# Threshold attention and a bilinear ffn: seven block products for the third column group as well

## The chip, the cores and the metric

The kernel runs on one core of a Trainium2 chip. The core has TensorE for matmuls (PE in the profile, its weight loads PEld), VectorE (DVE), ScalarE (ACT), GpSimd (POOL) and SyncE (SP), whose queue issues nearly all DMAs here; 16 DMA engines move the data. [...] The metric is the time of one execution on the device in microseconds, the median of several runs.

## The reference

```python
batch, n_heads, seq, head_dim = (8, 8, 576, 64)        # q, k, v in fp32; tau = 0.02
scores = scale * q @ k.T
thresh = max(scores) - tau                              # per row
scores = where(scores >= thresh, scores, -1e9)
attn = exp(scores - max(scores)) / (sum(...) + 1e-9)
x = (attn @ v), heads side by side                      # (4608, 512)
a = x @ w_a                                             # w_a, w_b: (512, 1536)
b = x @ w_b
out = (a * b) @ w_out                                   # w_out: (1536, 512)
```

All inputs and the output are fp32.

## The kernel before, in words

**Attention.** The 64 heads are worked on in 32 pairs (`pairs`, four to a batch). A pair's 576 query rows are five *units*: four of 128 rows and a tail of 64 (both heads in one tile). One pass of the main loop over `g` is a *slot* and starts one unit: `scores` (L386, TensorE) into two PSUM tiles, their row maxima on VectorE (L393), then in `weigh` the exponential on ScalarE (L414) and on VectorE the mask with the sum (L417), which is the last reader of the two score tiles. The weights are normalised on ScalarE (L436), transposed in blocks of 32 on VectorE (`turn_blocks`, L480), written to DRAM and read back in another order (`turn_back`; `swap`, `tw` and `wT` in the profile). Three slots behind its unit (`PV_LAG`), the product with v is made (`weighted`, L520) into one PSUM tile, and copied into `x`, transposed (L527, L528).

**The ffn.** A *block* is 256 rows of x (two halves of each batch, and a tail block out of four batches: 18 blocks). `x` and `xs` (the same with the two 64-row halves of the partitions exchanged, by GpSimd, `exchange`) feed matmuls of 64x64 quadrants, four of which make one product. The first layer has the 1536 columns of w_a and w_b in three column groups of 512 (`NG`). For the last two groups (`SEVENS = 2`) the block product of two 2x2 matrices (columns of x's rows, halves of w_a beside w_b) is formed from seven products in place of eight (`sevens_of`, L649 on): sums of weight blocks are made once (`first_sums`, GpSimd, L641), differences of x blocks for each block (`x_sums`, L550, four a tile, on GpSimd). The products accumulate in PSUM: a tile `a` through products 1, 6, 7 and 4 (between them ScalarE copies the running value out, L698, L705, L710), `b` for product 2 (read at L702), then `b` for 5 and 3 (L719, L714); products 4 and 3 end in VectorE's and GpSimd's multiplications (L723, L646). For the first group the four plain steps (column tile 0 or 1, w_a or w_b, `plain`, L753; read out by ScalarE at L759 and VectorE at L761) stand between them: the first three behind products 6, 7 and 5, the last at the end. A block's whole first layer is a generator that yields after every few matmuls. The second layer (L810) uses seven products too.

**PSUM.** `banks()` hands out one of four tiles of two banks each. Scores take two, pv one, an ffn product one; a tile comes free when its last reader is done.

**The order of the work** is written out by hand. The slot's program issues scores, then `advance(...)` for a share of the ffn's columns (`PORTIONS` 0.3, 0.35, 0.15, 0.2 of the slot's `pace`), with the other steps between: behind the first portion `weigh`, behind the second `weighted`, if one is due. `pace` spreads the waiting blocks (`backlog()`, `cost()` columns each) over the slots until the next block arrives. `keep_order` makes every engine follow the program's order. `make_room` runs the ffn on until a product is far enough from its ends before pv takes a PSUM tile, and `make_x` until an x tile is free (`XT_BUFS`, tag `xT`, which also holds the raw weights at the start). `exchange_blocks` turns a complete x into a block when no first layer is running.

**DMAs.** From slot 41 on DMAs are posted to a list (`post`, `bulk`), which `passed` empties by TensorE's progress (`PUMP` columns for each `PART` elements, `pump`); groups with the keys `tw` and `wT` go ahead of others of about the same slot, and `flush` issues what is needed now. v is loaded a slot ahead of a pair's first unit into one of four buffers (`load_v`), q and k a few slots ahead. The weights come at the start, `RAWS` pieces at a time plus as many as there are places in `extra`, and are converted from their 64-bit form in the first 15 slots.

**Weight sums.** From slot 22 on (`g > first[HP] + 1`), one `first_sums` is issued at the end of each slot, six in all; a block gets its x differences if `state["first"]` has reached that count when `exchange_blocks` takes it. The fourth sum of each group is made in place when the first such block starts.

Of the kernel before, what the change touches and what calls it, by code (L numbers as in the profile page):

```python
# [24 lines left out]
XT_BUFS = 7  # L25
# [9 lines left out]
RAWS = 4  # L35
# [19 lines left out]
def kernel(  # L55
# [83 lines left out]
    def post(key, *moves):  # L139

        if not state["paced"]:
            for move in moves:
                nc.sync.dma_start(*move)  # L143
        else:
            at = len(bulk)
            if key[0] in ("tw", "wT"):
                while at and bulk[at - 1][0][0] not in ("tw", "wT") and bulk[at - 1][1] >= state["slot"] - 1:
                    at -= 1
            bulk.insert(at, (key, state["slot"], moves))
# [50 lines left out]
    def load_v(i, again=False):  # L200
        b, hp = pairs[i]
        if not again:
            loaded[i]["v"] = loads.tile([P, NSLOT, D], FP32, tag="vm", bufs=HP, name="vm")
# [47 lines left out]
    more_sb = more_u32.bitcast(FP32)  # L251

# [73 lines left out]
    rooms = [t.rearrange("p (n w) -> p n w", n=NR) for t in rooms]  # L326
    load_rows(0, "q", rooms[0])
# [217 lines left out]
    def x_sums(x):  # L545

        t = x_tile("xU").rearrange("p m (k n) -> p m k n", k=2)
        b11, b12, b21, b22 = (x[:, k * 2:k * 2 + 2, n * P:(n + 1) * P] for k in range(2) for n in range(2))
        for m, a, b in ((0, b12, b11), (1, b22, t[:, 0]), (2, b22, b12), (3, b21, t[:, 1])):
            nc.gpsimd.tensor_tensor(t[:, m], a, b, op=ALU.subtract)  # L550
        return t

    def exchange_blocks():
        while complete and not state["layer"] and not blocks:
# [5 lines left out]
            blocks.append(((x, xs) + ((x_sums(x), x_sums(xs)) if state["first"] >= 3 * SEVENS else ()), what))  # L560
# [70 lines left out]

    def first_sums(n, group):

        quarter = [w[:, NG - 1 - group].rearrange("p (z y e) w -> p z y (e w)", z=2, y=2)[:, :, y]
                   for w in (wa_sb, wb_sb) for y in range(2)]
        s1, s2, s4 = ((first_sb, more_sb)[group][:, m * QUARTER:(m + 1) * QUARTER].rearrange("p (z w) -> p z w", z=2)
                      for m in range(3))
        a11, a12, a21, a22 = quarter
        out, a, b, op = ((s1, a21, a22, ALU.add), (s2, s1, a11, ALU.subtract), (s4, a12, s2, ALU.subtract),
                         (a21, a11, a21, ALU.subtract))[n]  # L640
        nc.gpsimd.tensor_tensor(out, a, b, op=op)  # L641

    def sevens_of(x, hg, plain):
# [5 lines left out]

        def quarter(n, y):  # L650
            return [[(wa_sb, wb_sb)[n][:, NG - SEVENS + g, k] for k in (2 * y, 2 * y + 1, 2 * y + HP, 2 * y + HP + 1)]
                    for g in range(SEVENS)]

        def s(m):
            return [[(more_sb, first_sb)[g][:, m * QUARTER + k * CH:m * QUARTER + (k + 1) * CH] for k in range(HP)]
                    for g in range(SEVENS)]
# [4 lines left out]
        def of_t(m):  # L661
            return [z[:, m, e] for z in (t, ts) for e in range(2)]

        products = {1: (quarter(0, 0), of_x(0, 0)), 6: (s(1), of_t(1)), 7: (quarter(1, 0), of_t(2)),
                    5: (s(0), of_t(0)), 2: (quarter(0, 1), of_x(1, 0)), 4: (quarter(1, 1), of_t(3)),
                    3: (s(2), of_x(1, 1))}
        nf = 2 * SEVENS
        whole = nf * HP * P

        def product(m, out, fresh, last):  # L670
            w, moving = products[m]
            left = whole
            for f in range(nf):
                g, y = f // 2, f % 2
                for k in range(HP):
                    for r in range(2):
                        rows = slice(r * D, (r + 1) * D)
                        for c in range(2):
                            w0 = y * P + c * D
                            nc.tensor.matmul(out[c * D:(c + 1) * D, r, f * P:(f + 1) * P],  # L680
                                             w[g][k][rows, w0:w0 + D], moving[k][rows],
                                             start=(fresh and k == 0 and f == 0),
                                             stop=(k == HP - 1 and f == nf - 1),
                                             skip_group_check=True)
                    left -= P
                    if left:
                        yield P, left, whole
# [4 lines left out]
        h0, h1 = (hg[:, :, :, n * P:(n + 1) * P].rearrange("p f r n -> p r f n") for n in range(2))  # L692
        third = [work.tile([P, nf * P], FP32, tag="osb", bufs=OSB_BUFS, name="u3") for _ in range(2)]
        done = P, 0, 0

        a = banks(nf * P, "pab")
        yield from product(1, a, True, False)
        nc.scalar.copy(h0, split(a))  # L698
        yield done
        b = banks(nf * P, "pab")  # L700
        yield from product(2, b, True, True)
        nc.vector.tensor_tensor(h0, h0, split(b), op=ALU.add)  # L702
        yield done
        yield from product(6, a, False, False)
        nc.scalar.copy(h1, split(a))  # L705
        yield done
        yield from plain(0)
        yield from product(7, a, False, False)
        for r in range(2):
            nc.scalar.copy(third[r], a[:, r])  # L710
        yield done
        yield from plain(1)
        yield from product(4, a, False, True)
# [425 lines left out]
```

## Time and profile before

| | |
|---|---|
| median of 3 runs | 1448.35 us (1442.43 to 1450.38) |
| profiled execution, first to last instruction (span) | 1439.3 us; the page gives no other time of it, so its own time is this span and what lies around it |
| median less span | 9.05 us |
| instructions | 77100 |
| TensorE busy | 1386.8 us, 34208 matmuls |
| VectorE, ScalarE, GpSimd busy | 1015.6, 683.9, 480.4 us |
| chain that ended last, by line | 27% L680 (seven products, first layer), 20% L810 (second layer), 19% L753 (plain products), 10% L386 (scores), 10% L520 (pv) |
| DMA | 223.25 MB, mean 155 GB/s |
| mean granted TensorE clock | 0.992 |

A group line of the profile reads: line, engine, operation, out<-in by the program's names, shapes, count; busy time and mean of one; idle time of the engine before it and what ended that. A timeline line has start, duration, engine, line, operation, tiles, shape and count; what stands in square brackets is idle time before it and who ended it. Matmuls overlap, so that the time of a stretch is taken from starts, not by adding durations.

### The profile page before, as it was taken

The page shows a single profiled execution, that of the slowest core. Times are in us where ns is not written, and L with a number is a line of the kernel's source. Part 1 is how long each engine was busy: PE and PEld are TensorE (multiplying, and loading weights), DVE is VectorE, ACT ScalarE, POOL GpSimd, SP SyncE. Part 2 cuts the span into 40 slices and gives each one's busy share as a digit, 9 for nine tenths or more (in the row PEclk, how much of TensorE's full clock was granted, in tenths as well). Part 3 has the DMA queues.
Part 4 walks back from the last instruction along what each step waited for, and adds up shares of the span by engine and source line. Part 5 has one row for each costly group of instructions (what it writes and reads, how often), then busy time and mean ns, then how long its engine had stood idle before and what let it go on. Part 6 is the DMA issues. An engine that isn't in the chain of part 4 may idle for free.

```text
span 1439.3 us, 77100 instructions
## 1 busy us (share of the span) xinstructions
PE 1386.8 (96%) x34208; PEld 1282.4 (89%) x34208; DVE 1015.6 (71%) x2244; ACT 683.9 (48%) x1244; POOL 480.4 (33%) x668
## 2 busy tenths in 40 slices
PE   6888999999999999999999999999999999999998
PEld 5777798988879889989999999898898989999998
DVE  6997778788767877676757786778867776755223
ACT  5876455545545454544444545344535454430110
POOL 2763713415060605132333333240506060605000
PEclk9899999999999999999999999999999999999999
DMA  9975667667755776567545677466755686450000
GB/s 210 252 227 141 173 173 191 182 171 192 202 137 153 176 201 159 152 160 189 147 125 137 159 186 203 118 171 149 207 135 142 164 217 167 121 160 18 3 18 17
DMA packets 327004, 223.25 MB, mean 155 GB/s; under 512 B 171536, under 2 KB 310800, under 8 KB 326672
## 3 DMA queue, kind: packets, MB, share of 16 engines
q1 hardware_dynamic: 324160, 217.74, 58.5%
q8 instruction: 269, 4.41, 1.3%
q10 hardware_dynamic: 2512, 0.59, 0.2%
q14 instruction: 63, 0.52, 0.1%
HBM read 128.58 MB, written 89.65 MB: 152 GB/s over the span
## 4 chain that ended last, share of the span: by engine, by line
PE 88%; DVE 4%; DMA 4%; issue 2%; SPq 2%; ACT 1%; DVEq 0%; ACTq 0%
PE pab L680 27%; PE po L810 20%; PE pab L753 19%; PE sc L386 10%; PE pv L520 10%; PE po L856 1%; DMA wT<-swap 1%; PE tp L461 1%; DVE mx L393 1%; DVE tw L480 1%; SPq L197 1%; DMA raw<-in_moe_w_a_dram 1%; SPq L143 1%; DMA raw<-in_moe_w_b_dram 0%; DVE tw L417 0%
## 5 line engine op out<-in xcount | busy, mean ns | idle before, releaser
L436 ACT ACTIVATE tw<-tw,rcp 128x576 f32<-128x576 f32 x272 | 197.8, 769 | 228.7 <-DVE rcp L430 228.6
L393 DVE TENSOR_REDUCE mx<-sc 128x1 f32<-128x576 f32 x288 | 206.1, 752 | 140.7 <-PE sc L386 115.6
L414 ACT ACTIVATE tw<-sc,bias,scalars 128x576 f32<-128x576 f32 x288 | 239.4, 831 | 9.8 <-ACT bias L413 0.2
L646 POOL TENSOR_TENSOR h<-h,u 128x512 f32<-128x512 f32 x28 | 35.1, 1276 | 604.2 <-DVE h L723 465.4
L810 PE MATMUL po<-wo_sb,h 64*64 64x256 f32 x3264 | 230.8, 377 | 0.0
L417 DVE SCALAR_TENSOR_TENSOR tw<-sc,thr,tw 128x576 f32<-128x576 f32 x288 | 222.6, 797 | 9.7 <-ACT tw L414 9.1
L386 PE MATMUL sc<-kT,qT 64*64 64x288 f32 x2016 | 198.1, 405 | 7.2 <-issue 2.9
L480 DVE STREAM_TRANSPOSE tw<-tw 128x576 f32<-128x576 f32 x272 | 196.0, 754 | 0.8 <-ACT tw L436 0.8
L810 PEld LDWEIGHTS po<-wo_sb,h 64*64 64x64 f32 x3264 | 178.7, 133 | 15.8 <-DVE h L723 0.3
L520 PE MATMUL pv<-wT,vm 64*64 64x160 f32 (+3 forms) x5184 | 181.7, 273 | 7.1 <-issue 4.3
L520 PEld LDWEIGHTS pv<-wT,vm 64*64 64x64 f32 x5184 | 167.7, 134 | 13.9 <-issue 6.8
L810 PE MATMUL po<-sums_u,h 64*64 64x256 f32 x2448 | 169.6, 377 | 0.3 <-DVE h L761 0.3
L779 POOL TENSOR_TENSOR h<-h 128x256 f32<-128x256 f32 x168 | 117.4, 733 | 119.8 <-PE po L810 116.1
L386 PEld LDWEIGHTS sc<-kT,qT 64*64 64x64 f32 x2016 | 119.5, 133 | 31.9 <-issue 10.6
L810 PEld LDWEIGHTS po<-sums_u,h 64*64 64x64 f32 x2448 | 132.2, 133 | 12.5 <-DVE h L761 1.2
L680 PE MATMUL pab<-xU,wb_sb 64*64 64x128 f32 x4096 | 138.5, 270 | 0.1
L680 PEld LDWEIGHTS pab<-xU,wb_sb 64*64 64x64 f32 x4096 | 131.0, 133 | 2.2 <-issue 0.5
L413 ACT ACTIVATE bias<-mx,scalars 128x1 f32<-128x1 f32 x288 | 83.3, 289 | 92.5 <-DVE mx L393 92.3
L680 PE MATMUL pab<-xS,wa_sb 64*64 64x128 f32 x2048 | 113.1, 270 | 1.2 <-issue 1.2
L753 PE MATMUL pab<-xS,wb_sb 64*64 64x256 f32 (+1 forms) x1536 | 102.9, 359 | 4.1 <-issue 4.1
L527 ACT COPY xT<-pv 128x128 f32<-128x128 f32 (+1 forms) x68 | 17.6, 259 | 187.2 <-PE pv L520 152.6
L753 PE MATMUL pab<-xS,wa_sb 64*64 64x256 f32 (+1 forms) x1536 | 101.4, 361 | 0.0
(138 smaller groups left out, 2427.7 us busy)
## 6 DMA issues: line engine op xcount, KB each, us to landing
wT<-swap SPq DMA_DIRECT2D x244, 288.0 KB, 3.8
swap<-tw SPq DMA_DIRECT2D x480, 144.0 KB, 2.9
vm<-in_v_dram SPq DMA_DIRECT2D x128, 72.0 KB, 2.8
swap<-tw SPq DMA_DIRECT2D x128, 72.0 KB, 3.1
kT<-in_k_dram SPq DMA_DIRECT2D x112, 72.0 KB, 3.1
wT<-swap SPq DMA_DIRECT2D x56, 144.0 KB, 2.6
out_dram<-kept SPq DMA_DIRECT2D x30, 256.0 KB, 3.5
qT<-in_q_dram SPq DMA_DIRECT2D x112, 40.0 KB, 2.6
```

Of the source, the lines that this page charges most:

```text
L386: nc.tensor.matmul(sc[j if u < NT else 0][to, c], qT[r, q0:q0 + D], kT[r, c * SH:(c + 1) * SH], start=True, stop=True)
L393: nc.vector.tensor_reduce(mx[:, c], sc[j], axis=AX.XY, op=ALU.max)
L413: nc.scalar.activation(bias[:, j:j + 1], mx[:, j:j + 1], AF.Copy, scale=e_nscale)
L414: nc.scalar.activation(wb[j], sb[j], AF.Exp, bias=bias[:, j:j + 1], scale=e_scale)
L417: nc.vector.scalar_tensor_tensor(out=wv, in0=sb[j], scalar=thr[:, j:j + 1], in1=wv, op0=ALU.is_ge, op1=ALU.mult, accum_out=sums[:, j:j + 1])
L436: nc.scalar.activation(w, w, AF.Copy, scale=rcp[:, j:j + 1])
L480: nc.vector.transpose(w, w)
L520: nc.tensor.matmul(pv[c * D:(c + 1) * D, y], vm[rows, s], wT[y](rows, s), start=(s == 0), stop=(s == NSLOT - 1))
L680: nc.tensor.matmul(out[c * D:(c + 1) * D, r, f * P:(f + 1) * P], w[g][k][rows, w0:w0 + D], moving[k][rows], start=(fresh and k == 0 and f ...
L753: nc.tensor.matmul(pab[c * D:(c + 1) * D, r], w[rows, f // n, k, fs + c * D:fs + (c + 1) * D], moving, start=(k == 0), stop=(k == H - 1))
L779: (nc.vector if state["over"] else nc.gpsimd).tensor_tensor(*a, **kw)
L810: nc.tensor.matmul(po[c * D:(c + 1) * D, r, y], ht[rows, t0:t0 + D], other[rows, f], start=(f == 0), stop=(f == NF // 2 - 1))
```

## The change

The first column group is now made from seven products as well. `sevens_of` has two streams, `main` (groups 1 and 2, PSUM tiles of 512 columns) and `side` (group 0, 256 columns), each with the seven steps of before and its own `a` and `b`, and they are woven: main 1, main 2, main 6, side 1, main 7, side 6, main 4, side 7, side 2, main 5, side 4, side 5, main 3, side 3. The plain steps in this layer are gone. The side stream's read-outs are one instruction each over 512 elements: three copies on ScalarE (h of 1, h of 6, u of 7) and five operations on VectorE (2, 4, 5, 3, and the multiplication behind 3); before, group 0 took two of each.

The sums of the third group have one buffer, `side_sb`. They are formed at start-up in three more slots (nine in all, `SUMS = 3 * NG`), each is stored to DRAM (`side_store`), and each block loads the three in turn, four DMAs of 128x256 fp32 each (`side_load`): the one for product 6 at the start of the layer, for 5 after side 6, for 3 after side 5. The key `s` is put ahead in the list like `tw` and `wT`, and a side product that needs a load flushes it.

To make room, `x_sums` writes one of its four differences into x itself and keeps three in a smaller tile of its own (tag `xU`, two buffers); `XT_BUFS` goes from 7 to 5, and a waiting block counts as two x tiles; `RAWS` goes from 4 to 3, while the new buffer is one more place for raw weights at the start. v has two buffers in place of four: it is loaded one slot behind a pair's first unit, and again two slots behind its third (`second`); for pairs 2 and 3 the first load goes into the `xU` tiles.

```diff
-XT_BUFS = 7
+XT_BUFS = 5
-RAWS = 4
+RAWS = 3
...
-            if key[0] in ("tw", "wT"):
-                while at and bulk[at - 1][0][0] not in ("tw", "wT") and bulk[at - 1][1] >= state["slot"] - 1:
+            if key[0] in ("tw", "wT", "s"):
+                while at and bulk[at - 1][0][0] not in ("tw", "wT", "s") and bulk[at - 1][1] >= state["slot"] - 1:
...
+        if 2 <= i < HP and not again:
+            spare = work.tile([P, 3, 2, P], FP32, tag="xU", bufs=2, name="vm")
...
+        elif i >= HP or not again:
+            loaded[i]["v"] = loads.tile([P, NSLOT, D], FP32, tag="vm", bufs=2, name="vm")
...
-        t = x_tile("xU").rearrange("p m (k n) -> p m k n", k=2)
+        t = work.tile([P, 3, 2, P], FP32, tag="xU", bufs=2, name="xU")
...
+    def side_load(m):
+
+        for k in range(HP):
+            part = slice(k * CH, (k + 1) * CH)
+            post(("s", m), (side_sb[:, part], side_store[m][:, part]))
...
+            if groups == (0,) and m in sums:
+                flush(("s", 3), ("s", sums[m]))
...
+            for f, k in ([(f, k) for f in range(nf) for k in range(HP)] if groups != (0,) else
+                         [(f, k) for k in range(HP) for f in range(nf)]):
...
+                elif m == 2:
+                    b = banks(size, "pab")
+                    yield from product(2, groups, b, True, True)
+                    nc.vector.tensor_tensor(h0, h0, split(b), op=ALU.add)
+                elif m == 6:
+                    a = held["a"]
+                    yield from product(6, groups, a, False, False)
+                    nc.scalar.copy(h1, split(a))
...
+                elif m == 4:
+                    a = held.pop("a")
+                    yield from product(4, groups, a, False, True)
+                    nc.vector.tensor_tensor(h0, h0, split(a), op=ALU.mult)
+                elif m == 5:
+                    b = held["b"] = banks(size, "pab")
+                    yield from product(5, groups, b, True, False)
...
+                if groups == (0,) and m in (6, 5):
+                    side_load({6: 0, 5: 2}[m])
...
+        main, side = stream((1, 2), h_main), stream((0,), h_side)
+        for of, m in ((main, 1), (main, 2), (main, 6), (side, 1), (main, 7), (side, 6), (main, 4), (side, 7), (side, 2),
+                      (main, 5), (side, 4), (side, 5), (main, 3), (side, 3)):
+            yield from of(m)
...
-            if g == first[p] - 1:
+            if g == (first[p] - 1 if p < HP else first[p] + 1) or p >= HP and g == second[p] + 2:
                 load_v(p)
...
-        if g > first[HP] + 1 and not converting and state["first"] < 3 * SEVENS:
+        if g > first[HP] + 1 and not converting and state["first"] < SUMS:
```

## The prediction

> **What bounds the kernel now.** I read the page first, then the waits of TensorE, then timelines of single stretches.
>
> ```profile
> span 1439.3 us, 77100 instructions
> ...
> PE 1386.8 (96%) x34208; PEld 1282.4 (89%) x34208; DVE 1015.6 (71%) x2244; ACT 683.9 (48%) x1244; POOL 480.4 (33%) x668
> ...
> PE 88%; DVE 4%; DMA 4%; issue 2%; SPq 2%; ACT 1%; DVEq 0%; ACTq 0%
> ```
>
> TensorE is busy for 96% of the span and makes up 88% of the chain that ended last. In windows of 72 us its busy time from 216 to 1368 us adds up to 1137 of 1152 us: only 15 us are idle there, at a granted clock of 1.00. So every matmul saved is worth its full time, and every new wait of TensorE costs its full time. The waits of TensorE between 200 and 1300 us say what such a wait would be:
>
> ```profile
> PE sc L386 <- DVE tw L417: 2.5, 3, 2.1
> PE pv L520 <- DVE kept L510: 1.5, 1, 1.5
> ```
>
> Columns: who waited for whom, us in total, times, longest. Both are waits for a PSUM tile that VectorE had not yet read out; there are hardly any, because a fourth tile was nearly always free.
>
> **The products themselves.** The timeline of TensorE around 740 us has both kinds of work back to back: one column group's part of one of the seven products (L680, 64 matmuls of 128 columns), and one plain step (L753, 64 matmuls of 256 columns):
>
> ```profile
> 737.71 0.27 PE L680 MATMUL pab<-xU,first_u 64*64 64x128 f32 x1
> ...
> 737.82 1.85 PE L680 MATMUL pab<-xU,first_u 64*64 64x128 f32 x60
> 739.46 0.38 PE L753 MATMUL pab<-xt,wa_sb 64*64 64x256 f32 x1
> ...
> 741.18 2.05 PE L753 MATMUL pab<-xS,wa_sb 64*64 64x256 f32 x32
> 742.91 0.54 PE L680 MATMUL pab<-xU,wb_sb 64*64 64x128 f32 x10
> ```
>
> 64 matmuls of 128 columns take 739.46 - 737.71 = 1.75 us (27.3 ns each); one plain step, 64 matmuls of 256 columns, takes 742.91 - 739.46 = 3.45 us. Removed per block: four plain steps (two column tiles, two weight matrices), 4 x 3.45 = 13.8 us. Added: seven products of 64, 7 x 1.75 = 12.25 us. Gain 1.55 us a block.
>
> [...]
>
> How many blocks? 16 of 18 use seven products now (16 multiplications at L723). The planner forms the x differences of a block only when all weight sums are issued. The six sums are issued one a slot from slot 22 (`g > first[HP] + 1`, with first[HP] = 20); the third block's x is complete in slot 30 (unit 27 plus PV_LAG), where no block is running, so it starts at once. With nine sums the ninth is issued at the end of slot 30, after that. So the third block falls back to plain products for all groups and loses the 2 x 1.55 = 3.1 us it has now. Sum on TensorE: 15 x 1.55 - 3.1 = **-20.2 us**. (If the block kept its sums it would be -24.8.)
>
> **PSUM.** There are four tiles. Scores take two, from the first score to the second masked multiplication (L417), 6.5 us in the median of a slot of some 8.4 us. Before, one accumulator is held (`a` through products 1, 6, 7, 4; then `b` through 5, 3), so one tile is spare. In the change the main and the side stream each hold one for most of the layer: `a` of main and `a` of side together from side 1 to main 4, `a` of side with main's `b`, then both `b`. Main 5 takes a new tile directly behind side 2, and side 5 directly behind side 4. With the scores holding two, the only candidate is the tile that VectorE must still read out. Behind it TensorE's whole queue waits: the products, the next scores and pv. What VectorE's latency is, the timeline of VectorE shows; the fifth product ends here at 614.8 us, just behind a unit's scores:
>
> ```profile
> 614.17 1.42 DVE L393 TENSOR_REDUCE mx<-sc 128x1 f32<-128x576 f32 x2 [1.38 <-PE pab L680]
> 615.63 0.23 DVE L394 TENSOR_SCALAR thr<-mx,scalars 128x2 f32<-128x2 f32 x1
> 615.76 1.43 DVE L480 STREAM_TRANSPOSE tw<-tw 128x576 f32<-128x576 f32 x2
> 617.12 1.25 DVE L719 TENSOR_TENSOR u<-u,pab 128x512 f32<-128x512 f32 x2
> 618.29 0.80 DVE L417 SCALAR_TENSOR_TENSOR tw<-sc,thr,tw 128x576 f32<-128x576 f32 x1
> ```
>
> The read-out stands behind two reductions and two transposes and ends 3.6 us after the product (617.12 + 1.25). Today nobody waits for it. I went through 37 such read-outs (L719, L761) between 300 and 1250 us, and took for each the time from the product's end to its read-out or to the first score tile's release, whichever is earlier, and zero if the scores were gone. Within 3 us of the scores' start: 2.8 us in the mean (12 rows); 3 to 6 us: 0.8 (16 rows); later: 0.1. The slot gives 30, 35 and 35% of its ffn columns to these stretches (PORTIONS), so 0.3 x 2.8 + 0.35 x 0.8 + 0.35 x 0.1 = 1.16 us for each of the two allocations. 13 of the 15 blocks run beside attention (the last two don't). Ends: 0, if a tile is always found, and 13 x (2 x 1.28 + 2 x 0.39) = 43 us: 1.28 is the plain mean of the 37, 0.39 their mean excess over 1.75 us, for the two allocations with one side product as cover (side 2 behind main 4, the second layer behind side 3). I take 0.85 for each of the 26, **+22 us**: a quarter below 1.16, because while TensorE waits VectorE runs ahead and the next read-out comes sooner (estimate).
>
> [...]
>
> **ScalarE's read-outs.** Product 7 adds into the tile that ScalarE still copies out after product 6 (L705), and 4 after 7 (L710). Now a plain step of 3.45 us covers each; then one side product of 1.75 us. The copies of L705 end 1.1 us after the product in 12 or so of 16 blocks, and 4.3, 2.8 and 3.1 us in three; L710's 1.2 us, and twice 3.1. Excess over 1.75: (4.95 + 2.7)/16 = 0.48 us a block, 6 us in 13. Bounds 0 (scores or pv fall between) and 6; I take **+4**.
>
> **Side loads.** Three times a block, four DMAs of 128 KB on SP's queue. The load for side 6 is posted at the block's start and that for side 5 five products ahead: both hidden. That for side 3 is posted when side 5 ends, with only main 3 (3.5 us) between. SP issues four DMAs in 1.75 us:
>
> ```profile
> 704.34 1.75 SPq L156 DMA_DIRECT2D swap<-tw  x4
> 708.41 3.49 SPq L156 DMA_DIRECT2D wT<-swap  x4
> ```
>
> and swap<-tw, 144 KB, the nearest size, lands 2.9 us after its issue. The quarters land 3.3, 3.8, 4.2 and 4.7 us after side 5; side 3 (k outermost) wants them at 3.5, 3.9, 4.4 and 4.8. That is in time by 0.1 to 0.2 us, and late by 1.75 or 3.5 us if a group of tw or wT issues stands ahead, unless scores or pv (1.4 to 2.4 us) fall between. Bounds 0 and 13 x 3.5 = 45; nearest to the plain case, 0.45 us a block: **+6**.
>
> **Together, with small answers.** VectorE gets five read-outs of some 0.67 us for two, +2 us a block, and ScalarE one of 0.58: 30 and 9 us beside 29% and 52% idle; their latency is in the terms above. The multiplication behind side 3 is hidden by the second layer's first product (48 matmuls of 53.9 ns, 2.6 us) against 1.4 us of VectorE; uncovered it would cost 1.4 us a block. v is loaded again for 28 pairs (112 more DMAs on SP), and 180 side loads come in: with 1152 packets a pair and 512 a load some 55,000 packets on 327,004, 17% more; the DMA share of some 0.65 in the windows from 216 us on becomes about 0.76. TensorE waits 0.4 us for a wT now; the loads stand three slots ahead of their use: 0, and 5 us at worst. The three stores of sums hold SP's queue behind GpSimd's sums of 2.4 us in slots 28 to 30, with kT, qT, tw and wT behind them: 0 to 7, I take **+1**. x_sums and the h product stay. XT_BUFS 7 to 5 leaves the same room beside a block (7 - 4 = 5 - 2 = 3); RAWS 3 and one more place in `extra` keep four pieces in flight: 0, at worst 3 us in the first 144 us, where TensorE is idle for 32.
>
> Sum: -20.2 + 22 + 4 + 6 + 1 = **+12.8 us** on a span of 1439.3, 1452.1. The median of the runs is 9.05 us above this span, and what lies around it doesn't change: 1448.35 + 12.8 = 1461.
>
> **The rivals.** *The spare tile isn't missed* (ends faster): the two allocations fall behind the scores' release, which 35% of the columns already do at 0.1 us. Then -20.2 + 4 + 2 remain, 1434; it decides when waits of all kinds stay below 13 us (20.2 less the 7.2 us that can be told). For it speaks that the planner shapes the phases; against it that the fifth product ended within 3 us of the scores in 7 of 12 blocks of that stretch. *The waits just pay for the gain*: 1441 to 1455. *The last side load is late as well*: banks at 1.28 us for each of the 26 (33) and 1.5 us a block for the load (20): -20 + 33 + 6 + 20, 1487; for it speaks the margin of 0.1 us, against it attention's work between. *Fewer blocks than 15*: each costs 4.7 us more; nothing after slot 31 speaks for it.
>
> **How the numbers follow.** Half a per cent, 7.2 us, is about what can be told from no change. Forecast 0.47, late loads 0.08: slower 0.55. Even 0.15. Spare tile 0.30: faster. The range goes from 1429 (the spare-tile case with the ScalarE copies hidden too) to 1483; about one in ten lies outside on each side. The forecast's own range is 1456 to 1475.
>
> **What the profile after would show.** 34208 + 15 x 192 - 384 = 36704 matmuls; 15 blocks with seven products, the third plain; TensorE's busy time down by some 20 us. New waits PE pab <- DVE at the starts of main 5 and side 5, some 20 us in total; PE pab <- ACT of a few us; PE pab <- DMA side_u before side 3. If the idle time from 216 us on stays near 15 us, the bank term was wrong and the time is near 1434. If idle is up by over 50 us, it is the loads.

## The result, and the profile after

The changed kernel takes 1549.55 us (median of four runs, 1540.53 to 1552.42) against 1448.13 us before: 1.0707 times the time before, 95% interval 1.0661 to 1.0754. It is 101 us slower. The forecast was 13 us slower, with a range that ended at 1483: the sign was right, the size wrong by a factor of eight. The two executions that were profiled, and that all step times below come from, differ by a little more: spans of 1439.3 and 1547.2 us, 107.9 us apart.

The page of the changed kernel has these lines for those shown of before:

```profile
span 1547.2 us, 82699 instructions
...
PE 1409.6 (91%) x36704; PEld 1258.8 (81%) x36704; DVE 1038.4 (67%) x2276; ACT 691.4 (45%) x1259; POOL 490.6 (32%) x674
...
PE 75%; DVE 8%; DMA 6%; issue 5%; ACT 2%; SPq 2%; POOL 0%; DVEq 0%; ACTq 0%
```

The count of matmuls is the forecast 36704: 15 blocks have seven products in all groups, and the third block is plain. In columns streamed from 216 us on, TensorE's work fell from 1167.1 to 1146.9 us at full speed, by the forecast 20.2 us. But its share of the chain fell from 88 to 75%, and idle time from 216 us on rose from 15.0 to 97.6 us. The waits of TensorE between 200 and 1400 us (who for whom, us in total, times, longest):

```profile
PE pab L701 <- issue: 25.5, 27, 2.7
PE pab L701 <- DVE h L752: 15.7, 7, 2.9
PE pab L701 <- DMA side_u<-side_store: 14.7, 8, 6.2
PE pab L701 <- DVE tw L424: 9.7, 8, 3.4
...
PE pab L701 <- ACT h L740: 1.5, 1, 1.5
```

L701 is the seven products, L752 the multiplication that reads the side stream's (or the main stream's) `a` behind product 4, L424 the mask that frees the scores, L740 a copy by ScalarE. All three forecast waits are there, and one that has no name: "issue". Two stretches of the timeline:

```profile
895.89 0.75 DVE L400 TENSOR_REDUCE mx<-sc 128x1 f32<-128x576 f32 x1
...
896.27 0.86 PE L701 MATMUL pab<-xU,wb_sb 64*64 64x128 f32 x24
...
896.81 1.43 DVE L487 STREAM_TRANSPOSE tw<-tw 128x576 f32<-128x576 f32 x2
...
898.16 1.25 DVE L758 TENSOR_TENSOR u<-u,pab 128x512 f32<-128x512 f32 x2
899.33 0.68 DVE L752 TENSOR_TENSOR h<-h,pab 128x512 f32<-128x512 f32 x1
...
900.06 1.69 PE L701 MATMUL pab<-xU,side_u 64*64 64x128 f32 x40 [2.93 <-DVE h L752]
...
1235.73 0.62 PE L701 MATMUL pab<-xS,first_u 64*64 64x128 f32 x16
1235.81 1.05 SPq L156 DMA_DIRECT2D wT<-swap  x2
1236.96 1.97 SPq L156 DMA_DIRECT2D swap<-tw  x4
1239.02 1.98 SPq L156 DMA_DIRECT2D side_u<-side_store  x4
...
1242.52 0.87 PE L701 MATMUL pab<-xT,side_u 64*64 64x128 f32 x9 [6.17 <-DMA side_u<-side_store]
```

In the first, side 4 has ended at 897.1 and side 5 wants a PSUM tile. The scores hold two, the main stream's `b` one, and the fourth is the one that side 4 has just filled. VectorE reads it only behind a reduction, two transposes and the read-out of main 5. In the second, main 3 ends at 1236.3 and side 3 wants its sums. Their four DMAs stand behind six others on SP's queue, are issued from 1239.02 on, and TensorE idles 6.17 us.

What follows such an idle time is seen in windows around the first stretch (window, length, busy time of PE with its matmuls, PEld, DVE, ACT, POOL; then the granted clock, the DMA share, GB/s):

```profile
892.00:897.00 5.00, 5.00 (x170) 4.64 (x160) 1.91 (x5) 2.40 (x4) 0.00 (x0) 1.00 0.97 265
897.00:900.00 3.00, 0.13 (x7) 0.00 (x0) 3.00 (x6) 1.18 (x3) 0.00 (x0) 1.00 0.94 271
900.90:904.20 3.30, 3.30 (x72) 3.30 (x68) 1.93 (x4) 0.00 (x0) 0.00 (x0) 0.50 0.49 82
904.30:908.00 3.70, 3.70 (x123) 3.29 (x117) 0.50 (x2) 0.27 (x1) 0.00 (x0) 1.00 0.56 134
```

After the idle 2.93 us the clock is granted at 0.50 for 3.4 us. The engine counts as busy there, with 72 matmuls in 3.30 us, where 123 are made in 3.70 us later. From 216 us to the end of the last products this happens ten times, for 37.5 us in all, so 18.8 us of work are lost; before it never happened in that stretch.

To see where the time went, I summed for each step the time from one matmul's start to the next one's, less 0.2117 ns a column (27.1 ns for 128 columns, the spacing in undisturbed stretches), with the scores and pv that fall into the step. Mean of the first 13 seven-product blocks, us of delay a block, worked out from the two traces:

| step | before | after |
|---|---|---|
| main 5, side 5 (each takes a tile) | 0.21 | 1.44, 2.55 |
| side 3 (late load) | none | 1.82 |
| main 7, main 4, side 7 | 0.26, 0.06, none | 0.75, 1.03, 0.60 |
| main 1, 2, 6, 3 | 1.49 | 2.03 |
| side 1, 6, 2, 4 | none | 1.47 |
| plain steps | 0.76 | none |
| second layer | 0.61 | 0.82 |
| sum | 3.39 | 12.50 |

13 x (12.50 - 3.39) = 118 us; less 20 us of work it leaves 98 of the 107.9 us between the two traces. The rest lies outside these blocks. Of the 118, the two tiles have 49, side 3 has 24, and all else together 46. The delay of a step includes the half clock that falls into it.

### The profile page after: what moved, and what is told of

Its sections match the earlier page's. It is cut to its first block, busy times and chain, and to the rows that moved or that the text cites. A ratio compares the mean times of both kernels' runs of the same rounds, so it can differ in the third digit from the quotient of the medians.

```text
span 1547.2 us, 82699 instructions
## 1 busy us (share of the span) xinstructions
PE 1409.6 (91%) x36704; PEld 1258.8 (81%) x36704; DVE 1038.4 (67%) x2276; ACT 691.4 (45%) x1259; POOL 490.6 (32%) x674
## 4 chain that ended last, share of the span: by engine, by line
PE 75%; DVE 8%; DMA 6%; issue 5%; ACT 2%; SPq 2%; POOL 0%; DVEq 0%; ACTq 0%
PE pab L701 31%; PE po L862 17%; PE sc L393 9%; PE pv L527 9%; PE pab L807 7%; DVE mx L400 2%; DVE tw L487 2%; DMA side_u<-side_store 1%; PE po L908 1%; DVE tw L424 1%; DMA kT<-in_k_dram 1%; DMA vm<-in_v_dram 1%; SPq L156 1%; DMA wT<-swap 1%; ACT tw L421 1%
## 5 line engine op out<-in xcount | busy, mean ns | idle before, releaser
L424 DVE SCALAR_TENSOR_TENSOR tw<-sc,thr,tw 128x576 f32<-128x576 f32 x288 | 223.7, 799 | 13.2 <-ACT tw L421 13.1
L862 PE MATMUL po<-wo_sb,h 64*64 64x256 f32 x3264 | 221.3, 379 | 0.7 <-DVE h L765 0.7
L862 PEld LDWEIGHTS po<-wo_sb,h 64*64 64x64 f32 x3264 | 159.8, 134 | 28.1 <-DVE h L765 1.0
L862 PE MATMUL po<-sums_u,h 64*64 64x256 f32 x2448 | 158.2, 377 | 2.4 <-DVE h L770 2.3
L393 PEld LDWEIGHTS sc<-kT,qT 64*64 64x64 f32 x2016 | 109.8, 133 | 47.5 <-issue 12.6
L701 PE MATMUL pab<-xS,wa_sb 64*64 64x128 f32 x2880 | 139.7, 270 | 0.3 <-issue 0.3
L862 PEld LDWEIGHTS po<-sums_u,h 64*64 64x64 f32 x2448 | 115.3, 133 | 26.5 <-DVE h L770 4.9
L701 PE MATMUL pab<-xT,wa_sb 64*64 64x128 f32 x2496 | 124.1, 270 | 3.4 <-DVE h L752 1.8
L701 PEld LDWEIGHTS pab<-xS,wa_sb 64*64 64x64 f32 x2880 | 114.3, 133 | 2.5 <-issue 1.4
L701 PEld LDWEIGHTS pab<-xT,wa_sb 64*64 64x64 f32 x2496 | 101.5, 133 | 6.3 <-DVE h L752 2.1
L701 PE MATMUL pab<-xU,wb_sb 64*64 64x128 f32 x2880 | 94.9, 270 | 6.6 <-issue 5.7
```

What stands on the lines that cost most here:

```text
L393: nc.tensor.matmul(sc[j if u < NT else 0][to, c], qT[r, q0:q0 + D], kT[r, c * SH:(c + 1) * SH], start=True, stop=True)
L424: nc.vector.scalar_tensor_tensor(out=wv, in0=sb[j], scalar=thr[:, j:j + 1], in1=wv, op0=ALU.is_ge, op1=ALU.mult, accum_out=sums[:, j:j + 1])
L862: nc.tensor.matmul(po[c * D:(c + 1) * D, r, y], ht[rows, t0:t0 + D], other[rows, f], start=(f == 0), stop=(f == NF // 2 - 1))
```

## The experiments

Three theories at the start: **B**, a PSUM tile is missing where main 5 and side 5 take one; **L**, the loads of side 3 are late; **M**, the edits for memory (v loaded twice, fewer x tiles) and the traffic of the loads slow down everything else.

Each interval compares a run with the kernel before as it ran beside it, at 1442.4 to 1443.9 us; beside the changed kernel it had 1448.1. A difference between a run and the changed kernel therefore carries some 6 us of doubt, and the step times of the traces say more. What is given per block is the mean of 13 blocks, as in the table.

**Order of side 4 and main 5.** The multiplication behind side 4 gets main 5 as cover before side 5 takes its tile.

```diff
-                      (main, 5), (side, 4), (side, 5), (main, 3), (side, 3)):
+                      (side, 4), (main, 5), (side, 5), (main, 3), (side, 3)):
```

> The changed kernel (1549.6 us) with one thing altered: side 4 stands ahead of main 5, so the woven order ends main 4, side 7, side 2, side 4, main 5, side 5, main 3, side 3. Side 5 then no longer takes a PSUM tile directly behind side 4, and main 5 has one side product between it and side 2. Theory B (a product that takes a PSUM tile finds none free, because main and side hold one each and the scores two): TensorE's loss at side 5, 2.5 us a block now, falls below 0.5 us, that at main 5 (1.4) to about 1; main 3 may lose 0.5 to 1 us more since its adds have less cover; 1515 to 1530 us in all. Theory L (late side loads, more DMA traffic) and theory M (fewer x tiles, v loaded twice, three raw tiles): no change beyond 5 us, 1545 to 1555.

1529.09 us, 1.0588 (1.0467 to 1.0708) of before, 20 us less than the change and inside B's forecast. The intervals of the two overlap, so that the size of the gain is not settled by this run; the steps are clearer. The delay at side 5 fell from 2.55 to 0.21 and at main 5 from 1.44 to 0.78 us a block. But main 3 rose from 0.60 to 1.60 (it now finds product 5 not yet read out), and side 3 from 1.82 to 2.94 us. Waits of TensorE in this kernel:

```profile
PE pab L701 <- DMA side_u<-side_store: 25.0, 9, 6.6
PE pab L701 <- issue: 20.0, 29, 3.0
PE pab L701 <- DVE u L758: 7.2, 9, 1.5
```

So B is right in kind: main 5 and side 5 lose 3.0 us a block less, 39 us in 13 blocks, and about half of that comes back as other waits.

**Without the side loads.** The sums of side 6, 5 and 3 are whatever was left in the buffer.

```diff
-            post(("s", m), (side_sb[:, part], side_store[m][:, part]))
+            pass
```

> The changed kernel without the 180 side loads: the side products read whatever lies in the one buffer, so products 6, 5 and 3 of the first column group are made from the wrong sums. Everything else stays. Theory L: side 3's loss (1.8 us a block, 23 us in 13 blocks) goes, and with the DMA traffic also the waits spread over the other products (about 40 us): 1485 to 1525. Theory B: only side 3's own loss goes, 1525 to 1535, and side 5 keeps its 2.5 us and main 5 its 1.4 us a block. Theory M: no change, 1545 to 1555.

1510.47 us, 1.0459 (1.0394 to 1.0524): 39 us less, inside L's forecast. Side 3's delay is gone (0.05 us a block), which is 23 of the 39; the rest came from the other steps, which the loads had also disturbed. The waits for tiles stayed:

```profile
PE pab L701 <- DVE tw L424: 17.3, 11, 2.7
PE pab L701 <- DVE h L752: 16.3, 7, 2.9
```

**Both.**

> The changed kernel with side 4 ahead of main 5 (as in the run with the altered order, 1529) and without the side loads (as in the run without them, 1510; products 6, 5 and 3 of the first column group are made from the wrong sums). If the two causes add up, side 3's loss of 2.9 us a block in the altered order goes as well: 1549.6 - 20.5 - 39 - 13 x 1.1 = 1476, so 1470 to 1492. If the missing tiles are all of it and the loads only fill up what the tiles cost, it stays at 1500 to 1512. What is left above 1448 then belongs to the other joins (main 7 and 4 behind side products, main 3 behind side 5, the second layer's start) and to the plain third block (3 us).

1483.75 us, 1.0292 (1.0241 to 1.0343): 66 us below the change, a little more than 20 + 39. Both causes are there side by side: against the run without loads (1510.47) the order alone now gives 27 us, well outside the spread of either. But 41 us above before remain, although 20 us of work are saved: 60 us of delay that neither B nor L explains. The waits of TensorE that are left:

```profile
PE pab L701 <- issue: 14.5, 23, 1.8
PE pab L701 <- DVE u L758: 8.1, 8, 2.0
```

By steps, main 3 has 15 of the 60 us: in this order it adds onto the tile of product 5 with side 5 alone between. The second layer, which waits for VectorE's last operations on h, has 8. What "issue" is comes below.

**Memory edits alone.** The first group is made by plain steps as before, without the third group's sums and loads; v twice, the smaller x tiles and the other edits stay.

```diff
-        main, side = stream((1, 2), h_main), stream((0,), h_side)
-        for of, m in ((main, 1), (main, 2), (main, 6), (side, 1), (main, 7), (side, 6), (main, 4), (side, 7), (side, 2),
-                      (main, 5), (side, 4), (side, 5), (main, 3), (side, 3)):
-            yield from of(m)
+        main = stream((1, 2), h_main)
+        for m in (1, 2, 6, 0, 7, 0, 4, 5, 0, 3):
+            yield from (main(m) if m else plain())
...
```

> The changed kernel without its side stream: group 0 is made by four plain steps again, in their old places between the main products (six sums, 16 blocks with seven products, no side loads). What stays of the change: 5 x tiles, the differences in a tile of their own with one of them written into x, 3 raw tiles, v with two buffers and loaded twice. The plain steps read the altered x, so group 0's values are not the reference's. Theory M: a good part of the 101 us stays, at least 30: above 1478. Theories B and L: 1446 to 1456, within 8 us of the kernel before, and its waits of TensorE near the 15 us of before.

1447.8 us, 1.0041 (1.0009 to 1.0073), some 6 us. M is out as a main cause. VectorE waits 26 us for q and k loads there and 14.5 us before, and TensorE idles during 1.5 of the 26.

**A tile held in the kernel before.** One more tile is taken ahead of product 4 and read by VectorE behind product 5. No work, load or order of the change is in it.

```diff
+        hold = banks(P, "hold")
+        for c in range(2):
+            nc.tensor.matmul(hold[c * D:(c + 1) * D, 0], wa_sb[0:D, 0, 0, 0:D], x[0:D, 0, 0:P], start=True, stop=True)
...
+        nc.vector.tensor_copy(scalars[:, 6:8], hold[:, 0, 0:2])
```

> The kernel before (1448.1 us) with one PSUM tile taken out of use for two products of each of its 16 blocks: a fifth user takes a tile ahead of product 4, two small matmuls write it, and VectorE reads two columns of it behind product 5. No other part of the change is in it. Two tiles are taken without a spare per block: the held one itself behind plain step 1, and that of product 5 directly behind product 4. Theory B: 2 x 1.0 to 2.0 us in 13 to 14 blocks beside attention, 1475 to 1505 us, with waits of TensorE at the start of product 5. Theories L and M: within 4 us of 1448.

1513.93 us, 1.0483 (1.0417 to 1.0549), 71 us slower and above B's forecast. The waits:

```profile
PE pab L757 <- DVE scalars L723: 21.4, 6, 3.7
PE hold L715 <- DVE h L765: 9.8, 4, 2.8
```

So a missing spare tile costs far more than its place in the sum suggested, in the kernel before as well. The place was not the forecast one: TensorE idles 7 us at the start of product 5, 13 us where the held tile is taken, and 24 us at the plain step behind product 5. While the scores hold two tiles, that step (L757) finds none until VectorE has read the held one, behind both read-outs of product 5. So three tiles in a block lack a spare here, not two, and the 71 us are no direct price for the forecast's term of 22. The half clock comes ten times here too, and takes 22 of the 71 us.

**The side stream in one tile.** Two halves of one tile serve as the side stream's `a` and `b`, so that main and side together hold no more than the four tiles allow; the order is made new so that a side step stands behind each main step.

```diff
-                    a = held["a"] = banks(size, "pab")
+                    if len(groups) > 1:
+                        a = held["a"] = banks(size, "pab")
+                    else:
+                        pair = banks(2 * size, "pab")
+                        a = held["a"] = pair[:, :, 0:size]
+                        held["b"] = pair[:, :, size:2 * size]
...
+        for of, m in ((main, 2), (side, 2), (main, 1), (side, 1), (main, 6), (side, 6), (main, 7), (side, 7), (main, 4),
+                      (side, 5), (main, 5), (side, 4), (main, 3), (side, 3)):
```

> The changed kernel with the side stream in one PSUM tile, products 1, 6, 7, 4 in one half of each bank and 5, 3 in the other, and a new weave: main 2, side 2, main 1, side 1, main 6, side 6, main 7, side 7, main 4, side 5, main 5, side 4, main 3, side 3 (ScalarE copies product 2 first, VectorE adds product 1). Nothing is left out. The side stream then takes one long-lived tile in place of two, every side product has a main product as cover, and the side loads for 5 and 3 have 8.7 us each. Theory B (tiles) with the loads: the loss of 12.5 us a block falls to 4 to 7, the kernel before has 3.4: 1450 to 1480. If the loads or the memory edits were the cause apart from side 3's wait, above 1510.

1532.32 us, 1.0629 (1.0558 to 1.07): a miss, and by the forecast's own words above 1510 speaks for the loads or the memory edits. The delays of the three steps went (main 5 0.61, side 5 0.06, side 3 0.15 us a block), and other waits took their place: main 3 now loses 3.05 us a block to a read-out, and the scores wait for a tile that VectorE has yet to copy into x:

```profile
PE pab L701 <- DVE u L765: 15.6, 9, 5.2
PE sc L393 <- DVE xT L535: 15.1, 5, 6.0
```

The longest of the first kind in the timeline:

```profile
649.74 1.36 PE L701 MATMUL pab<-xU,wb_sb 64*64 64x128 f32 x38
...
654.30 0.78 DVE L361 STREAM_TRANSPOSE kT<-kT 128x576 f32<-128x576 f32 x1 [2.41 <-DMA vm<-in_v_dram]
655.01 1.25 DVE L765 TENSOR_TENSOR u<-u,pab 128x512 f32<-128x512 f32 x2
...
656.31 0.92 PE L701 MATMUL pab<-xT,more_u 64*64 64x128 f32 x12 [5.21 <-DVE u L765]
```

Product 3 adds onto the tile that L765 still has to read behind product 5, with only side 4 (1.75 us) between. And VectorE itself stood for 2.41 us at a transpose whose data was late. From 216 to 1300 us it waits 48 us for loads in this kernel (35 in the changed kernel, 14 before), and TensorE idles during 12 of them. So the late loads have a part in this miss; how large it is was not tested.

**Two weight sums a slot** in that kernel, so that the third block has seven products as well.

```diff
-            first_sums(state["first"] % 3, state["first"] // 3)
-            state["first"] += 1
+            for _ in range(2 if state["first"] < SUMS - 1 else 1):
+                first_sums(state["first"] % 3, state["first"] // 3)
+                state["first"] += 1
```

> As the run with the halved side tile, and two weight sums a slot, so that all nine are issued by slot 26 and the third block, which starts in slot 30, gets its seven products: 16 blocks in place of 15. 3.1 + 1.55 us less on TensorE than with the halved side tile alone, so 2 to 7 us below it; at least 36704 + 384 + 192 = 37280 matmuls.

1523.84 us, 1.057 (1.0504 to 1.0637), 8.5 us below the kernel with the halved tile, somewhat more than the forecast 2 to 7, with two runs each that spread over 6 to 7 us, and 37280 matmuls. The planner's reading of the third block was right; its price is small against the rest.

**A read-out without cover**, in the kernel before: the plain step between products 5 and 3 comes behind product 3. No more tiles are held.

```diff
-        yield from plain(2)
         yield from product(3, b, False, True)
...
-            yield from plain(rest[3:])
+            yield from plain(rest[2:])
```

> The kernel before, with one plain step moved: the one that stood between product 5 and product 3 comes behind product 3. No work, tile, load or buffer is changed, and no more tiles are held than before; product 3 now adds into its tile with nothing between it and VectorE's read-out of product 5. In the trace of before this read-out ends 3.0 us after the product in the mean of the 13 blocks beside attention (39.5 us together) and 1.4 us in each of the last three, 43.7 us in all; the plain step (3.45 us) hides nearly all of it there. Theory C (a read-out without cover costs TensorE its whole latency, whatever the tiles do): less what the scores and pv cover now and then and what VectorE gains by running ahead, 25 to 45 us, and some more where the wait is over 2 us and the clock falls to half: 1470 to 1500 us, waits of PE for DVE at product 3 of 25 to 45 us, around 3 us each. Theory T (only a missing tile costs much; read-outs are taken up by other work in the queue): within 8 us of 1448.

1497.97 us, 1.0374 (1.0343 to 1.0404), 54 us slower. Theory C holds, near the top of its range. Waits of TensorE, and one of them in the timeline:

```profile
PE pab L680 <- DVE u L719: 39.5, 13, 4.6
```

```profile
631.24 1.42 DVE L393 TENSOR_REDUCE mx<-sc 128x1 f32<-128x576 f32 x2 [1.38 <-PE pab L680]
632.70 0.23 DVE L394 TENSOR_SCALAR thr<-mx,scalars 128x2 f32<-128x2 f32 x1
632.83 1.43 DVE L480 STREAM_TRANSPOSE tw<-tw 128x576 f32<-128x576 f32 x2
634.19 1.25 DVE L719 TENSOR_TENSOR u<-u,pab 128x512 f32<-128x512 f32 x2
...
635.49 1.13 PE L680 MATMUL pab<-xT,more_u 64*64 64x128 f32 x16 [3.65 <-DVE u L719]
```

The wait is the whole latency: the read-out ended 39.5 us behind the product in the 13 blocks of the trace of before, and 38 us of idle time stand at product 3 of these blocks now. No gain from "VectorE runs ahead" is seen. The half clock overlaps with 20 us of delay there: each us waited cost half a us more.

**The clock by itself.** TensorE makes equal streams of matmuls and waits between them for a chain of VectorE operations.

```diff
+            for m in range(BUSY):
+                r, c = m // 2 % 2, m % 2
+                nc.tensor.matmul(t[c * D:(c + 1) * D, r, 0:N], w[r * D:(r + 1) * D, c * D:(c + 1) * D],
+                                 u[r * D:(r + 1) * D, :], start=(m < 4), stop=(m >= BUSY - 4))
+            nc.vector.tensor_scalar(u, t[:, 0, 0:N], 1 / (BUSY // 4), None, op0=ALU.mult)
+            for _ in range(chain - 1):
+                nc.vector.tensor_tensor(u, u, u, op=ALU.mult)
```

> None of the reference's work: TensorE alone makes 300 matmuls of the plain step's form (64x64 weights, 256 columns, some 16 us), VectorE reads the sum and makes a chain of 1 to 14 small operations, and the next 300 matmuls wait for the chain's end; each length five times, so 70 idle gaps of TensorE from some 0.4 to 5 us, the output is filled with ones. Theory G (TensorE's clock is halved by the gap itself): as in the traces so far, gaps below 1.5 us are followed by a half clock in at most one of twenty, gaps of 2 to 2.5 us in about half, gaps over 3.5 us always; each time for 3.4 us or twice that. Theory N (the halved clock comes from something else in the kernel, such as the load on the other engines at that moment): no half clock, or one that doesn't go by the gap's length.

(The trace has two records for each matmul of the program, so a stream is 600 records and 32.6 us.) Five streams of one row, each with the idle time ahead of it:

```profile
635.16 32.61 PE L59 MATMUL sums<-u,w 64*64 64x256 f32 x600 [1.54 <-DVE u L64]
669.77 32.61 PE L59 MATMUL sums<-u,w 64*64 64x256 f32 x600 [2.01 <-DVE u L64]
704.85 32.61 PE L59 MATMUL sums<-u,w 64*64 64x256 f32 x600 [2.47 <-DVE u L64]
740.38 34.29 PE L59 MATMUL sums<-u,w 64*64 64x256 f32 x600 [2.93 <-DVE u L64]
778.06 34.29 PE L59 MATMUL sums<-u,w 64*64 64x256 f32 x600 [3.39 <-DVE u L64]
```

After 2.93 us of idle time the same stream takes 1.68 us more. Of all 70 gaps (one execution), none of the 16 below 2.0 us was followed by the half clock, 2 of 10 between 2.0 and 2.5 us, 4 of 5 between 2.8 and 3.0, and all 39 above 3.2; from 5 us on it always lasted 6.8 us in place of 3.4. Theory G holds.

**The waits without a name.** "issue" at L701 is 25.5 us in the changed kernel, some of it in the middle of a product (2.67 us at 380.53, 2.50 us at 722.34), where no tile and no operand is new. For each idle time over 0.3 us with no named releaser (216 to 1300 us) I looked at the packets of the instruction queue that feeds TensorE (206 packets of 16 KB in this stretch). In the changed kernel 17 of 28 end 1.2 to 1.7 us behind the end of such a packet, 16.6 us together; of the 37 idle times with a named releaser 3 do. Before it is 2.5 us, with the memory edits alone 3.0, and without the side loads still 10.2. (Four of the 28, 10.0 us, stand at side 5's first matmul and look like waits for its tile; one of them is among the 17.) A kernel with long streams of matmuls, with and without DMAs beside them, tells whether that is cause or chance:

```diff
+PHASES = tuple((load, cols, again) for again in range(2) for load in (None, "large", "small") for cols in (256, 128))
...
+        for m in range(COUNT[cols]):
+            r, c = m // 2 % 2, m % 2
+            nc.tensor.matmul(t[c * D:(c + 1) * D, r, 0:cols], w[r * D:(r + 1) * D, c * D:(c + 1) * D],
+                             u[r * D:(r + 1) * D, 0:cols], start=(m < 4), stop=(m >= COUNT[cols] - 4))
```

> None of the reference's work: TensorE alone makes long streams of matmuls with nothing to wait for, 100 us each, by turns of 256 columns (the plain step's form, 54 ns a record) and of 128 columns (the side products' form, 27 ns), each once without DMAs, once beside 200 loads of 128 KB in pieces of 1 KB, and once beside 50 loads of 128 KB in pieces of 128 bytes, all twice; the output is filled with ones. In the changed kernel 17 of 28 idle times of TensorE in the middle of its work that no engine explains (16.6 us of 29.7) end 1.2 to 1.7 us after the end of an instruction packet on the queue that feeds TensorE; in the kernel before it is 2.5 us. Theory F (TensorE runs out of instructions, which small matmuls use up twice as fast, when their fetch is held up by DMAs): idle times of 0.4 us and more within the streams of 128 columns beside DMAs, ending 1.2 to 1.7 us after such a packet; at most a few in the streams of 256 columns, and hardly any without DMAs. Theory N (the neighbourhood is chance, and something else of the kernel makes these waits): no idle time over 0.3 us within any stream.

Windows inside the first phases with loads (large pieces with 256 and 128 columns, small pieces with 256 and 128), and the second round's 128 columns without loads; columns as above without ScalarE's:

```profile
215.00:316.00 101.00, 101.00 (x1876) 71.60 (x1872) 0.30 (x4) 0.00 (x0) 1.00 0.80 239
342.00:447.00 105.00, 95.97 (x3309) 90.56 (x3305) 0.00 (x0) 0.00 (x0) 1.00 0.69 204
460.00:563.00 103.00, 103.00 (x1876) 67.81 (x1872) 1.22 (x9) 0.00 (x0) 0.98 0.45 66
570.00:680.00 110.00, 101.27 (x3559) 97.34 (x3555) 1.22 (x9) 0.00 (x0) 1.00 0.37 59
...
787.00:892.00 105.00, 103.85 (x3732) 101.81 (x3728) 0.00 (x0) 0.00 (x0) 1.00 0.02 5
```

The timeline of TensorE in the small-piece phase:

```profile
580.98 3.72 PE L73 MATMUL sums<-u,w 64*64 64x128 f32 x128 [0.85 <-issue]
585.28 3.72 PE L73 MATMUL sums<-u,w 64*64 64x128 f32 x128 [0.57 <-issue]
```

Theory F holds. With 256 columns TensorE is never idle. With 128 columns and no DMAs it loses 1 us in 105, and beside DMAs 9 in 105 or 110; in the second round of phases it is 4.8 and 6.2 us. The idle times stand between runs of 128 matmuls, which with their weight loads are 256 instructions, one 16 KB packet for them (the run with equal streams has 328 such packets for 84,000 matmuls and weight loads, 256 for each). In the four phases beside DMAs 32 of them are over 0.3 us, at 116 packets, and each of these ends 1.2 to 1.65 us behind a packet's end. By that, TensorE has run out of instructions there. The longest is 1.1 us: waits as long as the 2.67 and 2.50 us in the changed kernel were not made here, and no run takes the fetch out of the whole kernel, so that its share there rests on where the idle times stand. (The row of 101.00 us shows that a DMA share of 0.80 does nothing to the large matmuls.)

## Why the prediction was wrong, step by step

Against 33 us of waits in the forecast's sum (22 + 4 + 6 + 1) stand 118 us in 13 blocks. The step that failed is the price of the waits: the terms for PSUM and for the side loads were too small, ScalarE's stood for the wrong cause, and the half clock behind a wait and the instruction fetch were in none.

- **Work, -20.2 us: right**, in columns, matmuls and blocks. But the sign "TensorE's busy time down by some 20 us" failed: it rose by 22.8 us. An engine at half clock counts as busy, which is 18.8 us of this. The other some 24 us (22.8 + 20.2 - 18.8) are, by estimate, waits that the records hide: a matmul's record lasts 0.27 us, while the next one starts 0.027 us later.
- **PSUM, +22 us (bounds 0 to 43): mis-sized, 49.** The places and the mechanism were right. Main 5 cost 1.23 us a block more, near the 1.16 of the prediction's own rows; taking 0.85, "because while TensorE waits VectorE runs ahead", was the first error (the run with product 3 uncovered shows the whole latency paid). Side 5 cost 2.55 us: both allocations were priced alike, by read-outs of the kernel before, but VectorE's queue is fuller behind side 4. In 6 of the 13 blocks main 5's two read-outs (1.25 us) still stand ahead of side 4's, and in the mean side 5 starts 1.8 us behind side 4, while main 5 starts 0.9 us behind side 2. The upper bound of 43 held only idle time. The idle time right before the two products is 40 us; the half clock inside side 5, 7 us, was in no term.
- **Side loads, +6 us (bounds 0 to 45): mis-sized.** Side 3 cost 24 us, and taking all loads away gave 39. The margin of 0.1 to 0.2 us counted a free queue; the stretch at 1235.81 shows six other DMAs ahead. The prediction had named that case, and then took a sum near the plain one. With such a margin the plain case was not the likeliest, and the prediction's rival of late loads (1487) had the better price.
- **ScalarE's read-outs, +4 us (bounds 0 to 6): the wrong cause.** TensorE waits only 2.2 us for the copies at L740 and L746. Yet the steps besides main 5, side 5 and side 3 lost 46 us in sum. Of this, some 10 us (12.1 in these steps, less 2.5 before) are idle times over 0.3 us at the ends of instruction packets; the half clock and late read-outs at other places have shares that were not told apart. No step of the prediction had the instruction fetch.
- **Small matmuls in place of large ones**: in the rows at 740 us two matmuls of 128 columns take 2 x 27.3 ns against 53.9 ns for one of 256, 1.3% more, but a plain step stands beside the small product there. Streams of small matmuls beside DMAs idled for 4 to 9% of the time in the last experiment. The price has to come from a stream, not from one product.
- **Small answers.** Memory edits were costed at 0 to 3 and 0 to 5 us, and measured at some 6: near enough. What they do to VectorE was not looked at: its waits for q and k rose from 14.5 to 35.1 us (216 to 1300 us). Only 3.3 us of that lie under an idle time of TensorE; what a late VectorE costs afterwards was not separated. The DMA share, forecast to go from 0.65 to 0.76, hardly moved: 0.63 before and 0.66 after in the mean from 216 to 1296 us, with 31,752 more packets in place of 55,000.
- **The signs**: "if idle is up by over 50 us, it is the loads" was too narrow. Idle time rose by 82.6 us, and loads were about a third of it (without them it is 25.5 us less).
- **The 9.05 us** between the median and the span were taken as what lies around the span. In every run on record an execution takes only 1.7 to 2.8 us more than its own span, so some 7 us of it are the difference between one execution and the median. The forecast's change of 12.8 us does not depend on it.

What stays open is how the 46 us of the other steps divide between fetch, half clock and read-outs; in the kernel with both repairs, of the some 60 us that are left, main 3 and the second layer have 23, and the fetch by the same count some 10 (13.2 less 2.5); the rest is not taken apart. None of the versions that kept the side stream came below the kernel before.

## What to carry to other kernels

Price a read-out or a missing PSUM tile by the latency behind the busiest stretch of the reading engine, take away only the cover that really stands between, and count half as much again when the wait is over 2 us, because here TensorE's clock fell behind it (56 us of delay for 38 us of idle time in the run with product 3 uncovered). Before a step of large matmuls is swapped for more but smaller ones, price the instruction fetch in a stream beside DMAs: here TensorE idled for 4 to 9% of the time at 128 columns and never at 256; a saving of an eighth of the work in one group (1.6 us a block here) is easily lost to it. The load that was in time by 0.1 to 0.2 us on a free queue, by estimate, stood behind six other DMAs in the stretch at 1235.81, and TensorE idled 6.17 us for it.

## What the runs showed of the hardware that was not expected

**The clock fell after short idle times.** In nine of the ten traces of whole kernels (all but the one with product 3 uncovered), from 216 us on, 5 of 236 gaps of TensorE between 0.5 and 1.5 us were followed by the half clock, 9 of 36 between 1.5 and 2.0, 15 of 33 between 2.0 and 2.5, 13 of 16 between 2.5 and 3.0, and 20 of 23 longer ones. It came some 1 to 5 us after the gap's start, lasted 3.41 us or twice that, and cost half of this. Of the 62 gaps that it followed, 42 were shorter than 3 us.

**TensorE ran out of instructions in streams of small matmuls.** In streams of 128-column matmuls (27 ns each) beside DMAs it idled 0.3 to 1.1 us at 32 of 116 blocks of 16 KB of instructions, and for less at others; at 256 columns never (busy in 101.00 of 101 and 103.00 of 103 us). Without DMAs beside it, the stream of 128 columns idled 1.15 us in 105.
